# RetNet attention into a SwiGLU FFN: unit 2's norm moved between the output products of units 1 and 0

## The chip, the cores and the metric

The kernel runs on one core of a Trainium2 chip. The metric is the device time of one execution in microseconds (us); the time of a kernel is the median of several executions. The engines are named as in the profile: PE is TensorE (matmul), PEld its weight load, DVE is VectorE, ACT is ScalarE, POOL is GpSimd, SP is SyncE, which here only issues DMAs. Each engine works through its own queue strictly in order; engines wait for each other by semaphores.

## The reference

All arrays are float32 in shape `(8, 8, 576, 64)` for q, k, v. The attention has a decay in place of a softmax, its output is brought into the form of 4608 tokens by 512 features, and a gated FFN with an RMS norm follows:

```python
def _attn_ref(q, k, v):
    scores = scale * np.matmul(q, k.transpose(0, 1, 3, 2))
    Dmat = np.where(rel >= 0, gamma[:, None, None] ** rel[None, :, :], 0.0)
    return np.matmul(scores * Dmat[None], v)

def _moe_ref(x, w_gate, w_val, w_out, rms_g):
    rms = np.sqrt(np.mean(x * x, axis=-1, keepdims=True) + 1e-06)
    xn = x / rms * rms_g
    g = xn @ w_gate
    silu = g * (1.0 / (1.0 + np.exp(-g)))
    return silu * (xn @ w_val) @ w_out
```

The FFN is 512 to 1536 (twice, gate and value) and 1536 back to 512.

## The kernel before

The work is cut in two ways. The attention has 32 jobs, one for each batch and pair of heads. The FFN has 12 units of 384 tokens. The whole order is written out by hand (`manual_schedule`): each engine gets its instructions in the order in which the program writes them, and the framework only adds the waits and picks the buffers.

**A job** runs in `slot(j)`: `values(j-1)` (scores times v of the job before), `scores(j)` and `states(j)` on PE, `weigh(j)` and `sums(j)` on DVE, and `carried(j-1)` (the running state times q, added to the values, then multiplied into the columns of a unit's x on DVE). Between `values` and `carried` there is a link through the GpSimd: `values` ends with a memset of a one-element tile `tick` on POOL (L359) that waits for the last matmul of `values`, and the first matmul of `carried` (L370) waits for that memset (L376). `prepare(j)` transposes q and k on DVE and scales v on ACT; `load_next(j)` issues the loads of job j+2 on SP. `following(j)` is the two together.

**A unit's norm** has four parts. `norm_0(u)` squares the four feature blocks on ACT (L432) and adds them on DVE (three adds, L438). `norm_1(u)` sums over partitions with three small matmuls into `ms` (L450), adds epsilon on DVE (L455) and takes the power -1/2 on POOL (L456). `diagonals(u)` makes three diagonal matrices on DVE (L463). `norm_2(u)` spreads them over the partitions with a matmul into `rb` (L474), scales the four blocks of x on DVE (L476), and for units from 2 on makes the four differences (L487) that the FFN's block products need.

**The FFN's products** use Winograd's form of Strassen's scheme: seven block products in place of eight, with sums and differences of the blocks of weights and activations. `up` does so for units 2 to 11; units 0 and 1 go through `up_plain`, with the plain weights, while the weights arrive. `across(u)` is the output product of a unit, a generator with one step for each of its seven products, in the order x, z, w, y, x, z, w (the second x, z and w add into the same PSUM bank; below x', z', w'). Its steps, counted by `i` where the loop around it enumerates them: 0 is x, with the copy `m1o` on ACT (L671) and a block sum (L641); 1 is z; 2 is w; 3 is y, with the adds `u2o` and `u4o` (L638) and the output block (1,1); 4 is x' with output block (0,0) and a block difference (L641); 5 is z' with (0,1); 6 is w' with (1,0). An output block is transposed on DVE (L651) and stored by eight DMAs on SP (L661). z' writes the bank that `u4o` reads; w' reads what the block difference of step 4 writes. The first `next` of `across` only makes two block differences on DVE.

**The stretch that matters** is the end of `start()`: the output products of units 1 and 0 and what lies between them and the loop over units 2 to 11. `combine(m)` makes the Strassen combinations of the weights for `up`, 12 operations of 128x512 on POOL (L811) for each of gate and value. `combine(1)` (value) writes memory that holds unit 1's activations, so it waits for the last product of `across(1)`; `combine(0)` (gate) writes memory in which the combined output weights of units 0 and 1 lie, so it waits for the products of `across(0)` that read them. `slot(9)` contains `values(8)` and `carried(8)`, and after it comes the first product of `up(2, 0, 0)`.

The tiles that matter: `temp` is a ring of six 128x384 tiles (squares, diagonals, and the partial results of the products); `banks` is a pool of five PSUM banks, which the products, `ms`, `rb`, `last` and `av` share.

Of the kernel before, what the change touches and what calls it, by code (L numbers as in the profile page):

```python
# [22 lines left out]
def _decay_tables(H, D):  # L23

    pairs = _gamma(H).reshape(H // 2, 2).T
    rows = np.repeat(pairs, D, axis=0)
    pos = np.arange(L)
    p = np.concatenate([pos, pos])  # L30
    gq = rows[:, :, None] ** (pos + L) / np.sqrt(D)
    t = pairs.T[None] ** -p[:, None, None], rows**L, gq, np.roll(gq, D, axis=0)
    return [np.ascontiguousarray(x).astype(np.float32) for x in t]


def _causal_table():

    return np.ascontiguousarray(np.tile(np.triu(np.ones((L, L), np.float32)), (2, 1)))
# [3 lines left out]
def kernel(  # L42
# [44 lines left out]
    def bank(name):  # L87
        return banks.tile([P, 512], F32, tag="b", name=name)

    def temp(name):  # L90
        return tmp.tile([P, U], F32, tag="t", name=name)
# [163 lines left out]
    def scale_v(j):  # L255
        d = st[j]
        hp = jobs[j][1]
        for e in range(2):
            for t in (d["v"][:, :, e], d["vt"][:, e]):
                nc.scalar.activation(  # L260
                    out=t, in_=t, func=AF.Copy, scale=gv[: t.shape[0], hp, e : e + 1]
                )
# [161 lines left out]
    def following(j):  # L424
        prepare_next(j)
        load_next(j)
# [3 lines left out]
    def square(u, c):  # L430
        t = temp(f"sq_{u}_{c}")
        nc.scalar.activation(out=t, in_=x_of[u][:, c], func=AF.Square)  # L432
        return t

    def gather(u, c, sq):

        if c:
            nc.vector.tensor_tensor(out=t_of[u], in0=t_of[u], in1=sq, op=ALU.add)  # L438
        else:
            t_of[u] = sq  # L440

    def norm_0(u):
        for c in range(NHP):
            gather(u, c, square(u, c))

    def norm_1(u):

        ms = bank(f"ms_{u}")
        for s in range(NS):
            nc.tensor.matmul(  # L450
                ms[:, s : s + 1], lhsT=t_of[u][:, s * P : s * P + P], rhs=mean_w,
                start=True, stop=True,
            )
        r = tmp.tile([P, NS], F32, tag="r", name=f"r_{u}", bufs=1)
        nc.vector.tensor_scalar(out=r, in0=ms[:, :NS], scalar1=EPS, scalar2=None, op0=ALU.add)  # L455
        nc.gpsimd.tensor_tensor(out=r, in0=r, in1=mhalf.to_broadcast([P, NS]), op=ALU.pow)  # L456
        t_of[u] = r

    def diagonals(u):
        r = t_of[u]  # L460
        t_of[u] = temp(f"diag_{u}")
        for s in range(NS):
            nc.vector.tensor_scalar(  # L463
                out=t_of[u][:, s * P : s * P + P], in0=ident, scalar1=r[:, s : s + 1],
                scalar2=None, op0=ALU.mult,
            )

    def norm_2(u):

        x = x_of[u]
        rb = bank(f"rb_{u}")
        nc.tensor.matmul(rb[:, :U], lhsT=ones, rhs=t_of[u], start=True, stop=True)  # L474
        for c in range(NHP):
            nc.vector.scalar_tensor_tensor(  # L476
                out=x[:, c], in0=x[:, c], scalar=rms_g[:, c : c + 1], in1=rb[:, :U],
                op0=ALU.mult, op1=ALU.mult,
            )
        if u < 2:  # L480
            return
        b11, b12 = x[:, :2, :HU], x[:, :2, HU:]
        b21, b22 = x[:, 2:, :HU], x[:, 2:, HU:]
        t = ffn.tile([P, 3, 2, HU], F32, tag="sums", name=f"sums_{u}")
        t2, t3, t4 = (t[:, i] for i in range(3))
        for o, a, b in ((t3, b22, b12), (b12, b12, b11), (t2, b22, b12), (t4, b21, t2)):
            nc.vector.tensor_tensor(out=o, in0=a, in1=b, op=ALU.subtract)  # L487

        t_of[u] = b11, b21, b12, t4, t2, t3, b22
# [248 lines left out]
    def load_chunks(n, queue=nc.scalar):  # L738

        nonlocal n_loads  # L740
        while n_loads < min(n, len(chunks)) and waits_at.get(spare(n_loads)) is None:
            load_chunk(n_loads, queue)
            n_loads += 1
# [90 lines left out]
    def weights(n):  # L834

        for _ in range(n):
            next(steps, None)

    def weights_to(n):

        while n_chunks < min(n, len(chunks)):
            next(steps)
# [3 lines left out]
    def start():  # L846

        h_of[0] = ffn.tile([P, NF, U], F32, tag="h", name="h_0")
        tables = list(zip((causal, gv, gc, gq, gx), (_causal_table(), *_decay_tables(H, D))))

        def table(i, queue):
            t, values_ = tables[i]
            src = nc.inline_tensor(values_, name=t.tensor.name + "_table")
            queue.dma_start(out=t, in_=src.ap())

        make_identity(nc, ident)
        nc.scalar.activation(out=tick, in_=mhalf[:1], func=AF.Silu)
        nc.vector.memset(ones, 1.0)
        warm = bank("warm")
        for _ in range(6):  # L860
            nc.tensor.matmul(warm[:, :P], lhsT=ones, rhs=ones, start=True, stop=True)
        first_places.update(find_places())
        load_chunks(1)
        for i in (1, 0, 2):
            table(i, nc.scalar)
        weights(3)
        for j in range(2 * NHP):
            load_first(j, {0: range(2), 1: range(2, H), NHP: range(H)}.get(j))
            if j == 1:
                table(3, nc.sync)  # L870
            load_chunks((1, 1, 1, 1, 2, 2, 2, 3)[j], nc.sync)
        table(4, nc.sync)
        nc.sync.dma_start(out=rms_g, in_=moe_rms_g.rearrange("(c p) -> p c", p=P))
        load_chunks(4, nc.sync)
        turn(0)
        scale_v(0)
        act(3)
        squares = []
        for j in range(2 * NHP):
            slot(j)  # L880
            if j + 1 < 2 * NHP:
                turn(j + 1)
            if squares:
                gather(*squares.pop())
            for i in ((1,), (2,), (3,), (4, 5), (6,), (7,), (), ())[j]:
                scale_v(i)
            if j:
                u, c = divmod(j - 1, NHP)
                squares.append((u, c, square(u, c)))
            act(1)  # L890
            if j == 5:
                norm_1(0)
            elif j == 6:
                norm_2(0)
            weights((2, 0, 0, 1, 1, 1, 1, 0)[j])
            if j == 4:
                gather(*squares.pop())
            elif j == 5:
                diagonals(0)
            act(1)  # L900
        gather(*squares.pop())
        load_qk(2 * NHP)
        load_kv(2 * NHP)
        made = combine_out()
        for m, g in [(m, g) for g in range(NG) for m in range(2)]:
            for u in range(2):
                weights_to(4 * g + 2 * m + 1)
                for i, _ in enumerate(up_plain(u, m, g)):
                    if not (u or m or g):
                        if i == 0:  # L910
                            values(2 * NHP - 1)
                            carried(2 * NHP - 1)
                            gather(1, NHP - 1, square(1, NHP - 1))
                        elif i == 1:
                            norm_1(1)
                        elif i == 2:
                            diagonals(1)
                        elif i == 3:
                            norm_2(1)
                    weights(2)  # L920
                    act(1)
                    if u and m and g == NG - 1:
                        weights_to(len(chunks))
                        next(made, None)
                    if i == 1:
                        weights_to(4 * g + 2 * m + 2)
        for _ in made:
            pass
        for blk, t in first_blocks.items():
            keep(blk, t)  # L930
        rest = across(1)
        next(rest)
        following(2 * NHP - 1)
        for _ in rest:
            pass
        rest = across(0)
        next(rest)
        combine(1)
        slot(8, rest=False)
        following(8)  # L940
        for i, _ in enumerate(rest):
            if i in (1, 2, 4):
                (norm_0, norm_1, norm_2)[i // 2](2)
                if i == 2:
                    diagonals(2)
        combine(0)
        slot(9)
        following(9)
# [20 lines left out]
    with tc.manual_schedule():  # L969
        start()  # L970
        for u in range(2, NU):
            for i in range(2 * NG):
# [6 lines left out]
                if i == 2 * NG - 1:  # L979
                    rest = across(u)  # L980
# [39 lines left out]
```

## Time and profile before

| | |
|---|---|
| median of 5 runs | 1155.76 us (1154.79 to 1159.49) |
| profiled execution, its time | 1155.06 us |
| its span, first to last instruction | 1153.3 us |
| DVE busy | 718.8 us (62%) |
| POOL busy | 51.5 us (4%) |
| mean granted TensorE clock | 0.996 |
| DMA | 125.42 MB, mean 109 GB/s |

The profile is of one execution. The table's shares are means over very different stretches: the POOL's 51.5 us lie almost all between 214 and 253 us. Where the changed statements stand in time: `across(1)` runs from 188.7 to 216 us, the attention matmuls of slot 8 until 217.3, `across(0)` from 217.3 to 250.7, slot 9 from there to 253.6, and the first `up` product of unit 2 follows. After that ten similar rounds of unit 2 to 11 fill the span to its end.

A line of the waits reads: engine, tile and line that waited, then what it waited for; the total in us, how often, and the longest. A line of the windows reads: the stretch, its length, then busy time and number of instructions of PE, PEld, DVE, ACT and POOL, the granted clock (1.00 is full speed), the DMA engines' share and GB/s.

### The profile page before, as it was taken

The numbers are of one execution on the slowest core, as the hardware profiler recorded it, in microseconds if no ns is written. First come the engines' busy times: TensorE is split into PE (matmuls) and PEld (weight loads), VectorE is DVE, ScalarE is ACT, GpSimd is POOL, SyncE is SP. The second block draws the span as 40 slices with busy tenths as digits, with TensorE's granted clock in tenths as the row PEclk, the third lists the DMA queues.
The fourth block names the chain that finished last, engine by engine and source line by source line (L and its number), as shares of the span: only waits on it lengthen the run. The fifth ranks groups of instructions, "written<-read, shape, count | busy, mean of one in ns | idle before, by whom it ended". The sixth has DMA issues, their size and how long they took to land.

```text
span 1153.3 us, 24803 instructions
## 1 busy us (share of the span) xinstructions
PE 1127.5 (98%) x10524; PEld 1054.0 (91%) x10524; DVE 718.8 (62%) x1420; ACT 243.7 (21%) x480; POOL 51.5 (4%) x74
## 2 busy tenths in 40 slices
PE   8899999999999999999999999999999999999998
PEld 7655557998999999999999999999999999999998
DVE  5789857675576575465765775465576566445352
ACT  5545541102201211111221120120220220120210
POOL 0000000570000000000000000000000000000000
PEclk9999999999999999999999999999999999999999
DMA  8764236324453556035345456306436503403304
GB/s 208 207 179 146 109 137 191 65 41 116 120 128 59 156 134 147 21 98 108 96 108 83 113 139 127 114 29 119 112 84 139 139 24 92 128 1 99 122 1 110
DMA packets 292943, 125.42 MB, mean 109 GB/s; under 512 B 270432, under 2 KB 275808, under 8 KB 292832
## 3 DMA queue, kind: packets, MB, share of 16 engines
q1 hardware_dynamic: 282688, 107.66, 38.3%
q10 hardware_dynamic: 10144, 16.16, 4.3%
q8 instruction: 83, 1.36, 0.5%
q14 instruction: 28, 0.23, 0.1%
HBM read 108.83 MB, written 14.94 MB: 107 GB/s over the span
## 4 chain that ended last, share of the span: by engine, by line
PE 88%; DVE 6%; DMA 2%; ACT 1%; issue 1%; SPq 1%; ACTq 0%; DVEq 0%; POOL 0%; POOLq 0%
PE x L507 14%; PE w L507 13%; PE z L507 13%; PE up L564 8%; PE xo L629 8%; PE wo L629 7%; PE zo L629 7%; PE y L507 7%; PE yo L629 4%; PE av L351 2%; PE av L370 1%; PE s L280 1%; PE s L300 1%; DMA w_gate<-in_moe_w_out_dram 1%; DVE sum L329 1%
## 5 line engine op out<-in xcount | busy, mean ns | idle before, releaser
L531 ACT COPY m<-x 128x384 f32<-128x384 f32 x60 | 28.7, 478 | 454.7 <-PE x L507 430.4
L629 PE MATMUL xo<-h,w_out 128*128 128x192 f32 x528 | 90.3, 328 | 0.0
L507 PE MATMUL w<-sums,w_val 128*128 128x192 f32 x480 | 88.7, 328 | 0.6 <-DVE c L514 0.3
L507 PE MATMUL z<-x,w_gate 128*128 128x192 f32 x480 | 87.9, 326 | 1.1 <-DVE u L514 1.1
L507 PE MATMUL x<-x,w_val 128*128 128x192 f32 x480 | 88.8, 328 | 0.0
L507 PE MATMUL x<-x,w_gate 128*128 128x192 f32 x480 | 88.6, 328 | 0.0
L507 PE MATMUL z<-x,w_val 128*128 128x192 f32 x480 | 87.8, 326 | 0.0
L507 PE MATMUL w<-sums,w_gate 128*128 128x192 f32 x480 | 87.8, 326 | 0.0
L629 PEld LDWEIGHTS xo<-h,w_out 128*128 128x128 f32 x528 | 85.9, 190 | 0.6
L629 PE MATMUL wo<-h,w_out 128*128 128x192 f32 x504 | 85.3, 326 | 0.0
L514 DVE TENSOR_TENSOR u<-m,y 128x384 f32<-128x384 f32 x60 | 33.1, 552 | 79.2 <-PE y L507 79.1
L629 PEld LDWEIGHTS wo<-h,w_out 128*128 128x128 f32 x504 | 82.5, 190 | 0.0
L507 PEld LDWEIGHTS w<-sums,w_val 128*128 128x128 f32 x480 | 79.2, 190 | 2.9 <-DVE c L514 2.9
L507 PEld LDWEIGHTS z<-x,w_gate 128*128 128x128 f32 x480 | 79.6, 190 | 1.4 <-DVE u L514 1.4
L507 PEld LDWEIGHTS x<-x,w_val 128*128 128x128 f32 x480 | 79.2, 190 | 0.6
L507 PEld LDWEIGHTS x<-x,w_gate 128*128 128x128 f32 x480 | 79.3, 190 | 0.5
L507 PEld LDWEIGHTS z<-x,w_val 128*128 128x128 f32 x480 | 79.7, 190 | 0.0
L507 PEld LDWEIGHTS w<-sums,w_gate 128*128 128x128 f32 x480 | 79.6, 190 | 0.0
L514 DVE TENSOR_TENSOR h<-u,w 128x384 f32<-128x384 f32 x60 | 33.0, 550 | 69.5 <-PE w L507 69.4
L526 ACT ACTIVATE h<-h 128x384 f32<-128x384 f32 x90 | 47.0, 522 | 90.0 <-DVE h L514 90.0
L564 PE MATMUL up<-x,w_gate 128*128 128x384 f32 x192 | 63.3, 488 | 0.9 <-DVE x L476 0.7
L564 PE MATMUL up<-x,w_val 128*128 128x384 f32 x192 | 62.7, 487 | 0.2 <-ACT w_val L572 0.2
(170 smaller groups left out, 1775.1 us busy)
## 6 DMA issues: line engine op xcount, KB each, us to landing
w_out<-w_blocks SPq DMA_DIRECT2D x70, 768.0 KB, 4.9
out_dram<-o SPq DMA_DIRECT2D x368, 24.0 KB, 1.6
qraw<-in_q_dram SPq DMA_DIRECT2D x96, 72.0 KB, 2.8
kraw<-in_k_dram SPq DMA_DIRECT2D x96, 72.0 KB, 2.8
k<-in_k_dram SPq DMA_DIRECT2D x48, 128.0 KB, 3.0
v<-in_v_dram SPq DMA_DIRECT2D x48, 128.0 KB, 2.9
w_out<-in_moe_w_gate_dram ACTq DMA_DIRECT2D x5, 1024.0 KB, 5.8
w_out<-in_moe_w_out_dram ACTq DMA_DIRECT2D x3, 1024.0 KB, 4.8
```

Of the source, the lines that this page charges most:

```text
L280: nc.tensor.matmul(s[side(odd), e, i * L : i * L + L], lhsT=d["kT"][side(e), c * L : c * L + L], rhs=d["qT"][side(e), c * L : c * L + L], ...
L300: nc.tensor.matmul(o[side(e)], lhsT=d["k"][side(odd), i, e], rhs=d["v"][side(odd), i, e], start=True, stop=True,)
L329: nc.vector.scalar_tensor_tensor(out=t[:, c], in0=t[:, c - 1], scalar=gc[:, hp : hp + 1], in1=part, op0=ALU.mult, op1=ALU.add,)
L351: mm = nc.tensor.matmul(av[odd][column(j, odd, e), i * L : i * L + L], lhsT=d["v"][side(odd), i, e] if c < NC - 1 else d["vt"][:, e], rhs= ...
L370: mm = nc.tensor.matmul(av[odd][column(j, odd, e), i * L : i * L + L], lhsT=d["sum"][side(e), c - 1], rhs=d["qT"][side(e), c * L : c * L + L],
L507: nc.tensor.matmul(ps[:, i * HU : i * HU + HU], lhsT=w_up[m][:, 2 * blk + c, cut], rhs=t_of[u][blk][:, c], start=(start and i == c == 0), ...
L514: nc.vector.tensor_tensor(out=o, in0=a, in1=pairs_of(ps), op=ALU.add)
L526: nc.scalar.activation(out=o, in_=c, func=AF.Silu)
L531: nc.scalar.copy(out=s1, in_=pairs_of(x_))
L564: nc.tensor.matmul(ps[:, :U], lhsT=w_up[m][:, 4 * half + c, i * P : i * P + P], rhs=x_of[u][:, c], start=(c == 0), stop=(c == NHP - 1),)
L629: nc.tensor.matmul(ps[:, i * HU : i * HU + HU], lhsT=a[:, c, i * P : i * P + P], rhs=rhs[:, c], start=(start and i == c == 0), stop=False, ...
```

## The change

In `across(1)`, whose steps had nothing between them, `norm_0(2)` now stands after step 1 (z), and `norm_1(2)` and `diagonals(2)` after step 3 (y). In `across(0)`, which had `norm_0(2)` after step 1, `norm_1(2)` and `diagonals(2)` after step 2 and `norm_2(2)` after step 4, only `norm_2(2)` is left, and it stands after step 2 (w).

```diff
         rest = across(1)
         next(rest)
         following(2 * NHP - 1)
-        for _ in rest:
-            pass
+        for i, _ in enumerate(rest):
+            if i == 1:
+                norm_0(2)
+            elif i == 3:
+                norm_1(2)
+                diagonals(2)
         rest = across(0)
         next(rest)
         combine(1)
         slot(8, rest=False)
         following(8)
         for i, _ in enumerate(rest):
-            if i in (1, 2, 4):
-                (norm_0, norm_1, norm_2)[i // 2](2)
-                if i == 2:
-                    diagonals(2)
+            if i == 2:
+                norm_2(2)
         combine(0)
         slot(9)
         following(9)
```

No instruction is added or left out. In POOL's queue the power of L456 moves from between the last of `combine(1)` and the first of `combine(0)` to ahead of `combine(1)`. In PE's queue the `ms` matmuls move from before y of `across(0)` to before x' of `across(1)`, and the `rb` matmul from before z' to before y of `across(0)`. In DVE's queue the three adds and the small operations move with them, and the four scalings and four differences of `norm_2` now stand before `u2o` and `u4o` of `across(0)` and no longer behind its step 4. SP's queue keeps its order.

## The prediction

> **What bounds the kernel now.** I read the page first (line 1, part 4), then the chain, the waits and the timeline between 186 and 264 us, where the changed statements run, then the granted clock in slices of one microsecond, and last the GpSimd's own timeline.
>
> From the page:
>
> ```profile
> PE 1127.5 (98%) x10524; PEld 1054.0 (91%) x10524; DVE 718.8 (62%) x1420; ACT 243.7 (21%) x480; POOL 51.5 (4%) x74
> ```
>
> TensorE is busy 98% of the span, so an edit gains only what it takes out of TensorE's pauses. The waits in 186 to 262 us (who waited <- for whom: total, times, longest):
>
> ```profile
> DVE diag L463 <- POOL r L456: 2.1, 1, 2.1
> PE ms L450 <- DVE sq L438: 2.7, 1, 2.7
> PE z L507 <- DVE u L514: 1.1, 1, 1.1
> PEld av L370 <- POOL tick L359: 0.6, 1, 0.6
> ```
>
> The second line is the pause that this change is about, the last two are pauses behind it. The chain of the same stretch (start, length, what):
>
> ```profile
> 227.21 1.55 DVE sq L438
> 228.86 1.45 DVE sq L438
> 230.39 1.44 DVE sq L438
> 231.83 0.14 issue
> 231.97 0.91 PE ms L450 x6
> 232.88 5.57 PE yo L629 x24
> 238.45 3.91 PE xo L629 x24
> ```
>
> Three adds of VectorE hold TensorE, and the product after them takes 5.57 instead of 3.91. The clock says why (the columns to be read are the window and PEclk):
>
> ```profile
> 230.00:231.00 1.00, 0.00 (x0) 0.00 (x0) 0.90 (x2) 0.00 (x0) 1.00 (x1) 1.00 0.82 169
> 234.00:235.00 1.00, 1.00 (x5) 1.00 (x4) 0.00 (x0) 0.64 (x3) 1.00 (x2) 0.50 0.00 0
> 237.00:238.00 1.00, 1.00 (x8) 1.00 (x8) 0.84 (x1) 0.00 (x0) 0.92 (x2) 1.00 0.00 0
> ```
>
> After the pause the granted clock is halved for some 3.4 us: 1.66 us lost. Last the GpSimd alone, 184 to 256 us:
>
> ```profile
> 214.61 19.69 POOL L811 TENSOR_TENSOR w_val<-w_val 128x512 f32<-128x512 f32 x12 [145.37 <-PE wo L629]
> 234.25 0.86 POOL L456 TENSOR_TENSOR r<-r,mhalf 128x3 f32<-128x3 f32 x1
> 235.09 17.81 POOL L811 TENSOR_TENSOR w_gate<-w_gate 128x512 f32<-128x512 f32 x12
> 252.84 0.09 POOL L359 MEMSET tick<- 1x1 f32 x1
> ```
>
> This decides: the GpSimd works without a gap from 214.61 to 252.84, and the `tick` at its end releases `carried(8)` (line 376), which stands before unit 2's first product. TensorE waits for it already today, by 0.6 us, with all its other delays.
>
> **The change part by part**, on the clock of this execution (span 1153.3, its time 1155.06). I call the seven products of each unit x, z, w, y, x', z', w'.
>
> *Squares and adds into `across(1)`.* Four squares on ScalarE, some 0.42 apart: it is free from 193.3 to 203.6. Three adds of 0.56 (the row's median): VectorE is free from 196.4 to 204.6, and the GpSimd works only from 214.6. Nothing on the path; without this cover 1.7 us.
>
> *`ms` behind `across(1)`'s y.* Unit 3 shows its price: the chain has 0.56 for `ms` and 4.01 for the following product in place of 3.90, so 0.67. From 204.3 on TensorE runs 0.67 later.
>
> *`r`, power, diagonals there.* VectorE reads `ms` after the transpose that ends at 206.9, waits about 1.0 for the power, and makes three diagonals of 0.28: until 209.1. Behind it stand the transpose of block (0,0), ready at 208.4, and the subtraction for w' (1.31), which ends near 211.0, before w' at 212.7. The GpSimd is idle then, its queue holds nothing before the 12 subtractions and sums of `combine(1)`, so the power costs nothing. SP: outputs are issued from 206.93 and keep their order; loads for job 9 were issued before 202.5.
>
> *Removed from `across(0)`.* From the end of w at 229.1 to y at 232.9: 3.8 us (pause and `ms`); then 1.66 of half clock.
>
> *`norm_2` two products earlier.* TensorE: w ends at 229.76 (+0.67), the broadcast into `rb` takes 0.65 as in unit 3, y starts at 230.4, x' at 234.3, z' could start at 238.2. On VectorE the four scalings (2.1 in today's chain) and four subtractions now stand ahead of `u2` and `u4`, and z' overwrites what `u4` reads. While the GpSimd works a subtraction takes 1.51 where units later it takes 0.56: start to start 1.55. So: scalings 230.6 to 232.7, subtractions to about 238.05, `u2` and `u4` at 0.59 each to 239.25. z' waits 1.1 us. Bounds: 0 (subtractions at 0.6) and 1.9 (the first waits for a whole GpSimd operation too). I take 1.1, the row of the same place. Then w' at 243.2 (its subtraction ends by 242.4) and the attention slot at 247.1, against 250.7 today: 3.6 us won so far. The slot's matmuls up to `carried` take 1.7, so TensorE stands at `carried` at 248.8.
>
> *Where the GpSimd is.* It starts when `across(1)`'s w' has read enough: 214.61 + 0.67 = 215.28. Undisturbed operations follow each other at 1.34 (1.27 each), 24 make 32.1. Today's 38.23 therefore hold 0.84 for the power and 5.3 of disturbance by VectorE's operations with two SBUF inputs. What is spared: the power, and 0.75 that the three adds cost. What stays: the large subtractions (L641) lengthen an operation to 2.26 to 2.42 (about 4.0 in all), unit 2's four subtractions cost 0.2 to 0.3 each. 215.28 + 32.1 + 4.0 + 0.9 = 252.3 as against 252.84. Bounds: 251.3 without the small disturbance, 255.2 if each of the four subtractions costs the full 1.0 of a large one. I take 252.2, their own rows. `carried` follows 0.14 later, at 252.3 instead of 252.98: **0.65 us won, not 4**. TensorE pauses 3.5 us before it.
>
> *After `carried`.* Today z's second product waits until 261.44 for `u`, with 8.46 from `carried`; VectorE made `weigh(9)` inside this time, the multiplications only began 1.6 after `carried`. With the pause `weigh(9)` is done before, and they can begin 0.8 after: VectorE allows 252.3 + 7.66 = 259.95; TensorE needs 7.23 (today 252.98 to 260.21), unless its clock is halved. The pause of 2.7 was followed by half clock, one of 1.78 at 275.5 wasn't; 3.5 lies above both. Bounds of its cost to TensorE: 0, and 1.66 as at 232.9; the second gives 261.2. I take 260.6, since part of the halved time may fall into the pause and 0.4 is covered by VectorE. So -0.8.
>
> [...]
>
> Later nothing absorbs or adds: after 262 us TensorE waits only 0.3 for `c`, 0.3 for `tick` and 3.0 for issue. The sum is 1155.06 - 0.8 = 1154.3 for an execution like the profiled one. That one lies 0.7 under the median of five (1154.79 to 1159.49); halfway between I put the median after: **1154.7**.
>
> **The rivals.**
>
> 1. The GpSimd doesn't bind. If `combine` ran ahead of TensorE, what is won is the pause and `ms` less `ms` (3.8 - 0.67), 1.66 of clock, 0.6 at `tick`, about 0.7 behind, less 1.1 at z': 5.0, so 1150.1 for the execution, 1150.5 for a median. For it: the wait for `tick` is only 0.6 today. Against it: 38 us without a gap in the GpSimd's timeline, and nothing that it works through gets shorter by more than 1.6.
>
> 2. The GpSimd gets later: unit 2's four subtractions meet `combine` at the full 1.0 each, the upper bound above. `tick` at 255.2, `carried` 255.3, then 7.66 and the rest of the half clock (1.2): 264.1 against 261.44, +2.7: 1157.8. For it: the large subtractions do cost 1.0. Against it: the same four cost 0.2 to 0.3 each at 246 to 251 us, also during `combine`. It decides from a `tick` at about 253.4 on.
>
> 3. It doesn't do what it says: the adds in `across(1)` come late and `ms` waits there. Against it: 6 us of free time on both engines. Then 1155.7.
>
> **How the numbers follow.** GpSimd binds near its present end: 0.70, with 1152.8 to 1156.5 as its own range (tick 251.3 to 252.9, clock 0 to 1.66, and the runs' spread). Rival 1: 0.12. Rival 2: 0.12. Rival 3: 0.06. The range reaches part of the way to rivals 1 and 2: 1151.3 to 1157.9. What a measurement here can tell from no change is about 0.3%, 3.5 us: faster than 1152.3 is rival 1 and little else, 0.13; slower than 1159.2 needs rival 2 beyond its price, 0.07; within, 0.80.
>
> **What would show it.** `ms` at 204 to 205 us without a wait; clock 1.0 through `across(0)`; y at 230.4; z' held by `u4o` for about 1 us; the last `combine` operation ending at 252 to 252.5; a wait of PE av L370 for POOL tick of about 3.5 us where 0.6 stood; half clock after it; z of the first up product at about 260.6. If `tick` comes before 250 or after 253.5, or TensorE doesn't wait for it, the prediction is wrong at its centre.

## The result, and the profile after

The changed kernel takes 1152.69 us (median of 39 runs, 1149.49 to 1155.59) where the kernel before, run beside it, takes 1155.2 (70 runs): ratio 0.9974, 95% interval [0.9967, 0.9981], 2 to 4 us less. The forecast was 1154.7, in a range of 1151.3 to 1157.9. The direction and the place where the gain stops were forecast; the gain is 2.5 us, of which the working has only the smaller part.

The profiled execution after took 1153.25 (span 1151.5). `across(1)` begins at 188.69 in the profile before and at 189.38 in the one after; ahead of it nothing was changed, and this point wanders from 187.6 to 192.9 over the ten profiles of this study. So I compare from there, with a plus sign. Waits of 186 to 262 us after (who waited <- for whom: total, times, longest):

```profile
PEld av L370 <- POOL tick L359: 3.3, 1, 3.3
PE av L370 <- POOL tick L359: 3.2, 1, 3.2
...
DVE diag L463 <- POOL r L456: 1.0, 1, 1.0
PE zo L629 <- DVE u4o L638: 0.8, 1, 0.8
```

The 2.7 us of `ms` are gone. In their place stand a new wait of 0.8 at z' and, at `carried(8)`, 3.2 where 0.4 stood, both named in the prediction. The GpSimd's timeline, 184 to 256 us:

```profile
207.72 0.85 POOL L456 TENSOR_TENSOR r<-r,mhalf 128x3 f32<-128x3 f32 x1 [137.91 <-DVE r L455]
215.98 19.27 POOL L811 TENSOR_TENSOR w_val<-w_val 128x512 f32<-128x512 f32 x12 [7.41 <-PE wo L629]
235.21 17.57 POOL L811 TENSOR_TENSOR w_gate<-w_gate 128x512 f32<-128x512 f32 x12
252.72 0.09 POOL L359 MEMSET tick<- 1x1 f32 x1
```

Again there is no gap from the first operation of `combine(1)` to `tick`. From the start of `across(1)`, `tick` moved from +64.16 to +63.33, 0.83 earlier, while TensorE would have been ready 4 us earlier. The clock after (window, length, busy times, PEclk, DMA):

```profile
250.00:251.00 1.00, 0.00 (x0) 0.00 (x0) 0.64 (x2) 0.00 (x0) 0.92 (x2) 1.00 0.34 53
254.00:255.00 1.00, 1.00 (x5) 1.00 (x4) 0.97 (x3) 0.00 (x0) 0.00 (x0) 0.50 0.18 27
258.00:259.00 1.00, 1.00 (x8) 1.00 (x7) 1.00 (x2) 0.00 (x0) 0.00 (x0) 1.00 0.32 49
```

The half clock has moved with the pause, from `across(0)` into unit 2's first products. The second z of that step starts at +72.39; before it was +72.76. So the stretch that the change touches has won 0.4 us. Counted from the start of `across(1)`, the two profiled executions end 2.5 us apart (+964.6 and +962.1); the other 2.1 us come later. The chain of waits before, from 264 us on:

```profile
275.19 0.35 PE av L370 x22
275.54 1.78 issue
277.32 0.38 PE av L370 x9
277.70 1.50 PE x L507 x8
```

and the same place after (slot 10, `carried(9)`):

```profile
275.41 0.47 PE av L370 x31
275.88 1.50 PE x L507 x8
```

A pause of 1.78 us, in which TensorE waited for nothing that the profile names ("issue"), is gone. Just ahead of these lines the two profiles lie 0.5 us apart, behind them 2.5 (x at +89.02 and +86.50): nearly all of the 2.1 us arise here. The pause lies behind instruction 5058 of TensorE's records; the others of its kind lie behind 1474 and 5569, multiples of 256 apart (256 x 14 and 256 x 2, to within one). In the instruction queue of the DMA records a packet of 16,384 bytes, 64 for each of 256 instructions, starts at 274.97 before and at 272.72 after (that queue has 83 packets in all, for 21,215 records of TensorE). So TensorE was, I infer, waiting for its next block of instructions. What may have stood in the way shows in SP's timeline before:

```profile
240.86 20.78 SPq L661 DMA_DIRECT2D out_dram<-o  x32
261.74 2.02 SPq L142 DMA_DIRECT2D qraw<-in_q_dram  x4
...
268.88 1.07 SPq L609 DMA_DIRECT2D w_out<-w_blocks  x2
```

and after:

```profile
241.03 18.00 SPq L661 DMA_DIRECT2D out_dram<-o  x32
259.14 2.01 SPq L142 DMA_DIRECT2D qraw<-in_q_dram  x4
...
266.28 1.07 SPq L609 DMA_DIRECT2D w_out<-w_blocks  x2
```

Unit 0's outputs take 2.8 us less to issue, since the last two blocks no longer wait behind `norm_2` on VectorE; the loads of job 11 and the first two fetches of output weights (768 KB each) follow earlier. The last of their packets starts at 275.25 before and at 272.34 after. The instruction block starts 1.6 us after TensorE began on the block ahead of it in the kernel before, and 0.9 us ahead of that beginning in the changed one. That the weights hold the block up is so far an inference from two profiles. It became theory 2, beside theory 1 (the GpSimd's queue sets when `carried(8)` begins).

### The profile page after: what moved, and what is told of

Read it like the earlier page. It is cut to its first block, busy times and chain, and to the rows that moved or that the text cites. A ratio compares the mean times of both kernels' runs of the same rounds, so it can differ in the third digit from the quotient of the medians.

```text
span 1151.5 us, 24802 instructions
## 1 busy us (share of the span) xinstructions
PE 1127.4 (98%) x10524; PEld 1054.6 (92%) x10524; DVE 716.1 (62%) x1420; ACT 243.8 (21%) x480; POOL 50.7 (4%) x74
## 3 DMA queue, kind: packets, MB, share of 16 engines
q8 instruction: 83, 1.36, 0.5%
## 4 chain that ended last, share of the span: by engine, by line
PE 91%; DVE 3%; DMA 2%; POOL 2%; ACT 1%; issue 1%; SPq 0%; ACTq 0%; DVEq 0%; POOLq 0%
PE x L507 14%; PE w L507 14%; PE z L507 13%; PE xo L629 8%; PE wo L629 8%; PE zo L629 8%; PE up L564 8%; PE y L507 7%; PE yo L629 4%; PE av L351 2%; PE av L370 2%; POOL w_gate L811 1%; PE s L280 1%; PE s L300 1%; DMA w_gate<-in_moe_w_out_dram 1%
```

## The experiments

Ratios are to the kernel before, run beside them on the same chip; the kernel before had medians of 1154.28 (25 runs) in the first four and 1154.47 (17 runs) in the rest. None of these kernels leaves anything out.

**`tick` ahead of most of `combine(0)`** (`split_after`), made from the changed kernel:

```diff
-    def combine(m):
-        for g in range(NG):
+    def combine(m, groups=range(NG)):
+        for g in groups:
...
-        combine(0)
+        combine(0, (0,))
         slot(9)
         following(9)
+        combine(0, (1, 2))
```

> The changed kernel, with only the first third of combine(0) (the four operations of group 0) ahead of slot 9 and the other eight behind it, so that tick stands behind 16 and no longer 24 combine operations. Nothing is left out. Theory 1 (the GpSimd's queue sets when carried(8) begins): the wait of PE av L370 for POOL tick falls from 3.2 us to under 0.5, the half clock after it (some 2 us in all) goes, and the second z of unit 2's first up step comes about 4.2 us earlier, bound by VectorE alone. Rival (TensorE would stand there anyway, for the sums on VectorE): the tick wait turns into a wait for DVE sum or DVE ret and the time stays within 1 us of the changed kernel. Theory 2 (TensorE's next block of instructions is fetched behind the fetch of output weights, which SP issues at a time that this edit hardly moves): TensorE now comes to slot 10 some 4 us earlier, at 271, before that weight fetch has ended at 272.3, and an issue pause of 2 to 4 us comes back at the same instruction (av L370 of slot 10) that had 1.78 us in the kernel before and none in the changed one; total then 1150.5 to 1152. Without theory 2 the gain stays whole: 1148 to 1149.

Measured: 1151.07, ratio 0.9972 [0.9961, 0.9982]. TensorE's waits from 186 to 310 us:

```profile
PE av L370 <- issue: 2.2, 1, 2.2
PE zo L629 <- DVE u4o L638: 0.8, 1, 0.8
PE z L507 <- DVE u L514: 0.5, 1, 0.5
```

The wait for `tick` is gone, `carried(8)` starts at +60.13 (3.35 earlier), the second z at +68.05 (4.3 earlier): theory 1 holds, and no other wait stood behind the GpSimd. But the whole kernel has hardly won: at slot 10 the issue pause is back with 2.23, and half clock follows it (the x product behind it takes 2.71 in the chain, where it takes 1.50 in the changed kernel). Both theories are needed for that.

**The same split in the kernel before** (`split_before`, same edit).

> The kernel before, with the same split of combine(0). Nothing is left out. Theory 1: there the GpSimd held carried(8) up by only 0.4 to 0.6 us, TensorE being late by itself for the ms pause, so the tick wait goes and the gain is 0.3 to 0.7 us: 1154.5 to 1155. Rival (the split is good in itself, whatever the order of the norm): it gains as much as in the changed kernel, some 4 us.

Measured: 1151.73, ratio 0.9979 [0.9968, 0.9989]: 2.4 us, not 0.3 to 0.7. This was a miss, and useful. The second z starts 1.1 earlier (+71.62), and the pause at slot 10 has gone as well (none over 0.6 us), which I had not counted; the one at slot 11 stays, with 1.58. VectorE in the kernel before:

```profile
247.16 1.51 DVE L487 TENSOR_TENSOR x<-x 128x384 f32<-128x384 f32 x1
248.71 1.51 DVE L487 TENSOR_TENSOR sums<-x 128x384 f32<-128x384 f32 x1
250.25 1.51 DVE L487 TENSOR_TENSOR sums<-x,sums 128x384 f32<-128x384 f32 x1
251.69 0.54 DVE L638 TENSOR_TENSOR c<-u2o,zo 128x384 f32<-128x384 f32 x1
```

and with the split:

```profile
246.39 0.56 DVE L487 TENSOR_TENSOR x<-x 128x384 f32<-128x384 f32 x1
246.99 0.56 DVE L487 TENSOR_TENSOR sums<-x 128x384 f32<-128x384 f32 x1
247.58 0.56 DVE L487 TENSOR_TENSOR sums<-x,sums 128x384 f32<-128x384 f32 x1
248.05 0.55 DVE L638 TENSOR_TENSOR c<-u2o,zo 128x384 f32<-128x384 f32 x1
```

The GpSimd is idle at 240 to 251 us here, so each difference takes 0.56 in place of 1.51, the output blocks leave earlier, SP issues the weight fetch at 265.28, and the instruction block (271.40) is there in time. This is the chain of theory 2 from its first link, without the change.

**Less weight traffic ahead of slot 10, in the kernel before** (`fetch121_before`):

```diff
-                if i in (1, 3):
-                    fetch()
-                    fetch()
+                for _ in range(({1: 1, 3: 2, 5: 1} if u == 2 else {1: 2, 3: 2}).get(i, 0)):
+                    fetch()
```

> The kernel before; for unit 2 only, the fetches of output weights go out as one after i=1, two after i=3, one after i=5 in place of two and two. Nothing is left out. Theory 2: at slot 10 the weight traffic ends 2.6 us earlier (272.6 in place of 275.2), the block of instructions for TensorE arrives in time, and the issue pause of 1.78 us before av L370 at 277 is gone, while the one of 1.24 us at 299 stays: 1153.2 to 1153.8. Rival (the pause is chance, or belongs to the number of instructions alone): it stays at 1 to 2 us, time within 0.5 us of the kernel before.

Measured: 1153.09, ratio 0.999 [0.9978, 1.0002]; in time it can't be told from no change. The pause can be told. The chain at slot 10:

```profile
276.24 0.47 PE av L370 x31
276.71 1.50 PE x L507 x8
```

31 matmuls in one piece where before 1.78 us lay between them. The one at slot 11 stayed (1.73). In this execution half clock lasted 6.83 us behind the `ms` pause and came again at 299.9, which hides the gain in its own time. The longer half clock also made everything 1.7 us later here, TensorE's work and SP's fetch alike (+81.85; +80.19 before), so the traffic is to be read against TensorE: the last weight packet starts 0.6 us before TensorE begins on the block ahead, where in the kernel before it starts 1.9 after that. The time supports theory 2 weakly, the chain does so plainly.

**More weight traffic ahead of slot 10, in the changed kernel** (`fetch31_after`, the same lines with `{1: 3, 3: 1}` for unit 2).

> The changed kernel; for unit 2 only, three fetches of output weights after i=1 and one after i=3. Nothing is left out. Theory 2: the weight traffic at slot 10 lasts 2.6 us longer, to 275, and the issue pause before av L370 of slot 10 comes back with about 2 us; the second one (1.25 us, slot 11) shrinks or goes, because its traffic ends 2.6 us earlier. Sum 0 to +1 us: 1152.7 to 1153.7. Rival (the block's arrival has nothing to do with the weights): both pauses as in the changed kernel, none at slot 10 and 1.25 us at slot 11.

Measured: 1150.02, ratio 0.996 [0.9948, 0.9973]. The chain at slot 10:

```profile
272.45 0.35 PE av L370 x23
272.80 1.42 issue
274.22 0.34 PE av L370 x8
```

The pause is back with 1.42, and the one at slot 11 is gone, as theory 2 has it; the last weight packet starts 1.2 us later than in the changed kernel, not 2.6. The time, expected at 1152.7 to 1153.7, is a miss: it came out lower. The interval overlaps that of the change, and why the median is lower stays open; of the profiled execution I can say why it was faster: the pause before `carried(8)` was 3.15 us again, but no half clock followed (second z at +71.11, not +72.39).

**`norm_2(2)` back at its old place** (`norm2_late`), in the changed kernel:

```diff
-            if i == 2:
+            if i == 4:
                 norm_2(2)
```

> The changed kernel with norm_2(2) back at its old place, behind step 4 of across(0); norm_0, norm_1 and the diagonals stay in across(1). Nothing is left out. Theory 1 (carried(8) begins when the GpSimd is through): the wait of z' for u4o (0.8 us) goes, TensorE stands at carried some 0.8 us sooner and waits the same time longer, tick lies within 0.4 us of where it is (63.3 us after across(1) begins): time within 0.7 us of the changed kernel. Rival (bringing norm_2 forward is what wins or costs): the time moves by the 0.8 us of the wait, tick and carried with it. Theory 2: output blocks (0,1) and (1,0) come some 4 us later than in the changed kernel, but SP still issues the last of them within 1 us of its time there, so the issue pause at slot 10 is 0 to 1 us.

Measured: 1152.86, ratio 0.9977 [0.9964, 0.999]. The waits of TensorE, 186 to 262 us, all of them:

```profile
PE av L370 <- POOL tick L359: 4.3, 1, 4.3
```

The wait at z' is gone and the one at `carried(8)` is longer by 1.1; `tick` is at +63.41 (+63.33 in the changed kernel). What TensorE wins ahead of `carried(8)` it waits there. Half clock lasted 6.83 us behind the longer pause (second z at +73.07). Slot 10 has no issue pause here either, although two output blocks stand behind `norm_2` again: SP has issued the outputs by +68.5, then waits until +69.8 for VectorE's transposes (L251), and issues the first weight fetch at +76.89, as in the changed kernel. That `across(0)` runs 3 us earlier is, then, enough to free slot 10, with `norm_2` at either place. So the second half of the change, moving `norm_2`, brings nothing as long as the GpSimd binds.

**Split and weights early** (`early_fetch`): the changed kernel with the split, and for unit 2 three fetches between `slot(9)` and `following(9)`, one after i=5.

```diff
         slot(9)
+        for _ in range(3):
+            fetch()
         following(9)
...
-                if i in (1, 3):
-                    fetch()
-                    fetch()
+                for _ in range(({5: 1} if u == 2 else {1: 2, 3: 2}).get(i, 0)):
+                    fetch()
```

> The changed kernel with combine(0) split (one group ahead of slot 9, two behind it) and, for unit 2, three fetches of output weights ahead of the loads of job 11 and one after i=5, so that no weight traffic lies near slots 10 and 11. Nothing is left out. Theories 1 and 2 together: no wait for tick, no issue pause over 0.7 us at slots 10 and 11, no half clock between 186 and 300 us; TensorE gains what the split gained (3.3 at carried) and doesn't give it back: 1.6 us under the split alone and some 3 to 4.5 us under the changed kernel, ratio to the kernel before 0.9935 to 0.9955. Rival (the pause at slot 10 is set by the number of instructions or by the loads of jobs, not by the weights): the pause of 2.2 us stays, ratio 0.997.

Measured: 1146.08, ratio 0.9926 [0.9909, 0.9943]. TensorE's waits, 186 to 310 us:

```profile
PE zo L629 <- DVE u4o L638: 0.8, 1, 0.8
PE z L507 <- DVE u L514: 0.5, 1, 0.5
```

No wait for `tick`, no issue pause over 0.6 us at slots 10 and 11, no half clock between 46 and 1144 us. The two waits together were worth a little more than the ratio of 0.9935 to 0.9955 that the theories said. The loads of job 11 now run while the block for slot 10 arrives (1043 packets of 128 bytes between +79 and +80), and it came in time: it's the weights and not the loads that held it up.

**And `norm_2(2)` at its old place** (`late_early`, the two edits above together).

> As the kernel with combine(0) split and the weights fetched early, and norm_2(2) back behind step 4 of across(0). Nothing is left out. Theory 1: once the GpSimd doesn't hold carried up, the 0.8 us that z' waits for u4o count, and the differences of norm_2 now run after the last operation of combine's first group, at 0.56 instead of 1.51 us: TensorE is at slot 9 0.8 us sooner, but the chain of VectorE behind carried (7.7 us) may take part of it back: 0 to 0.8 us faster than with norm_2 early, ratio 0.993 to 0.9955. Rival (VectorE's chain alone sets the first z of unit 2, and norm_2 late makes it later): 0.5 to 1 us slower.

Measured: 1145.76, ratio 0.9917 [0.9902, 0.9932], the fastest here. TensorE's waits, 186 to 310 us:

```profile
PE z L507 <- DVE u L514: 0.5, 1, 0.5
```

One wait of 0.5 us is left of all that stood in this stretch. `carried(8)` is at +59.04, 1.08 earlier than with `norm_2` early, and the last matmul ends 0.8 earlier; the intervals of the two ratios overlap, so in time the step is likely and not settled. The ratio lies under the 0.993 to 0.9955 expected, as that of `early_fetch` did.

**The kernel before, once more** (`before_again`).

> The kernel before, unchanged, for a second profile of it. Theory 2: the issue pause before av L370 of slot 10 is there again with 1.5 to 2 us, since the weight traffic ends again about 86.5 us after across(1) begins and the block of instructions starts to arrive only then. Rival (that pause was chance): it is absent or at another place. The half clock behind the ms pause may last one window of 3.4 us or two, or be missing, by where the windows lie.

Its one time is 1158.84, with `across(1)` beginning at 192.91, 4.2 later than in the first profile. From there on the two agree: `carried(8)` at +64.30 in both, the second z at +72.75 and +72.76. The pause at slot 10 is there, with 1.27, a little under the 1.5 to 2 expected (the last weight packet starts at +86.06; +86.57 in the first profile).

Theory 2 in one table. Times are from the start of `across(1)`; "needed" is where TensorE reaches the end of its block at slot 10, "block before begun" is where it started on the 256 instructions ahead of that.

| kernel | block before begun | last weight packet starts | block starts to arrive | needed | pause |
|---|---|---|---|---|---|
| before | +84.7 | +86.6 | +86.3 | +86.9 | 1.78 |
| before, again | +84.7 | +86.1 | +85.7 | +86.8 | 1.27 |
| after | +84.2 | +83.0 | +83.3 | +86.2 | none |
| split_after | +80.0 | +83.8 | +81.9 | +82.2 | 2.23 |
| split_before | +83.5 | +84.1 | +83.3 | +85.5 | none |
| fetch121_before | +86.4 | +85.8 | +85.6 | +88.3 | none |
| fetch31_after | +83.1 | +84.1 | +84.3 | +85.2 | 1.42 |
| norm2_late | +84.9 | +83.0 | +84.5 | +86.8 | none |
| early_fetch | +80.0 | +77.2 | +79.0 | +81.9 | none |
| late_early | +78.9 | +72.8 | +78.5 | +81.1 | under 0.1 |

Where the last weight packet starts before TensorE begins on the block ahead (after, fetch121_before, norm2_late, early_fetch, late_early), the new block starts to arrive 0.4 to 1.1 us before that beginning; where it starts later, from 0.2 before (split_before) to 1.9 after it (split_after). Wherever TensorE paused, at slot 10 or 11, it went on 2.2 to 2.5 us after the packet started; where the packet started 2.2 us or more ahead of need there was no pause.

## Why the prediction was right, and where it was not

*Squares, adds and `ms` in `across(1)`.* As predicted: squares at 193.9, adds of 0.55 to 0.56 until 198.9, `ms` at 204.99 without a wait, diagonals done at 209.3.

*The pause and its half clock.* y of `across(0)` starts at +41.72; predicted +41.7.

*z' held by `u4o`.* Predicted 1.1, measured 0.8.

*The GpSimd.* `tick` was predicted at +63.5 (252.2) and came at +63.33; the wait for it 3.5, measured 3.16. Rival 1, that the GpSimd doesn't bind, is refuted by `split_after`, which moved `carried(8)` by 3.35 with an edit of its queue alone. Rival 2, the full 1.0 for each of the four differences, is refuted by the operations beside them, which took 1.46 to 1.58 where undisturbed ones take 1.27. Rival 3 is refuted by `ms`.

*After `carried`.* The bounds from the start of `across(1)` were +71.3 without and +72.5 with half clock; measured +72.39 with it, and +71.11 without it in `fetch31_after`. I took +71.9 on the ground that part of the halved time would fall into the pause; in the profile after, all of it fell behind (the pause ended at 252.86, half clock lasted from 253.94 to 257.36).

*What failed* is the sentence "Later nothing absorbs or adds: after 262 us TensorE waits only 0.3 for `c`, 0.3 for `tick` and 3.0 for issue." I read the 3.0 for issue as a fixed part of the kernel. It was two pauses for instruction blocks, 1.78 and 1.24, and the first one depended on when SP issued the weight fetch, which depends on when VectorE is through with `norm_2` (+63.1 before, +49.4 after, +58.3 in `norm2_late`, which was early enough). Later, 2.1 us were won where the sum has none, more than five times what was won up to there. My reading of SP's queue stopped at order: "outputs are issued from 206.93 and keep their order" is true, and the times at which `across(0)`'s outputs left were never worked out, though the profile before shows 20.78 us for these 32 issues where the 32 of `across(1)` took 16.57.

The forecast was a little small, then, because a second mechanism was left out, not because the first was wrong. That the stated range holds the time is in part luck: 1152.69 lies just under the 1152.8 to 1156.5 that the prediction gave its central case, in the room that was left for rival 1, and rival 1 didn't occur. The 0.8 predicted was not measured where it was expected either: there it was 0.4, since all of the half clock counted.

## What to carry to other kernels

When a wait on the main engine is taken away, look for the next thing that it waits for on the same stretch, and above all at an engine that shows 4% of the span and is busy without a gap just there: a one-element memset at the end of the GpSimd's queue took back 3.2 of 4 us. A pause marked "issue" in a burst of small matmuls need not be a constant (at slot 10 it was 1.78, 1.27, 2.23, 1.42 us or none): find out whether it lies at a multiple of the instructions in one packet (here 256 in 16,384 bytes), and keep bulk DMA traffic away from the time when that packet should start. Here it started 2.2 to 2.9 us ahead of need in the kernels without a pause. Two such limits hide each other: here the split of `combine(0)` gave nothing that can be measured on top of the change (0.9972 and 0.9974), the split together with the earlier weights 0.9926, some 5.5 us more; the earlier weights alone weren't tried.

## What the runs showed of the hardware

*The clock's windows.* In the profiles before and after, every stretch of half clock but the last of each, which runs past the kernel's end, lasted 3.41 or 6.83 us. Within each profile they begin on one grid: before at 37.96, 232.52 and 1150.70, which are 57 and 269 times 3.4133 apart; after at 8.18, 38.90, 253.94 and 1151.65, which are 9, 63 and 263 times 3.4133 apart. Call a piece of that grid a window. The windows in which TensorE was busy for less than 40% (before: 32, 20 and 23%, from 34.55, 229.11 and 1147.29; after: 22, 32 and 0%, from 4.77, 250.53 and 1148.24) were all followed by half clock. Of those from 43 to 61%, one of 48% was (after, from 35.49); 43 and 54% (after) and 60 and 61% (before) were not. Behind a busier window at full clock, half clock never began in these two. The 1.78 us pause at slot 10 of the kernel before lies mostly in the window of 60%, the 2.7 us pause at `ms` in the one of 20%. The length of a pause alone doesn't tell: the one of 2.23 in `split_after` was followed by half clock, the one of 3.15 in `fetch31_after` was not (clock 1.00 in 252:253 and 254:255).

*VectorE and GpSimd together.* In the profiles before and after, a 128x384 add or difference of VectorE with two SBUF inputs (L438, L487) takes 0.55 to 0.56 while the GpSimd is idle. While the GpSimd works through `combine`, the adds took 1.43 to 1.62 and the differences 1.51, the first difference 0.60 to 0.75; operations of the same size with one input in PSUM (L476, L638) took 0.54 to 0.61 then too. Beside those adds and differences the GpSimd's 1.27 (128x512) became 1.45 to 1.58. For each of the larger differences (L641, 128x1152, 1.31 to 1.36 alone) that ran during `combine`, one operation of the GpSimd took 2.26 to 2.42.

*Instruction blocks.* The instruction queue (q8 of the page) shows 83 packets of 16,384 bytes in each of the two profiles, for 21,215 and 21,213 records of TensorE: 256 for a packet, to within 0.2%. At slot 10 the packet's start lay 0.9 us before TensorE began on the block ahead in the profile after and 1.6 us behind that beginning in the profile before; the last weight packet, on another queue (q1), started at +83.0 and at +86.6 (the other kernels are in the table above). An attention slot holds 280 TensorE instructions and takes 2.32 us without a pause (slot 10 of the profile after), about the 2.2 to 2.5 us that lay between a late packet's start and TensorE's going on; the late blocks of this stretch showed in slots 10 and 11.
